# Decay attention and two MLPs on one core: natural keys of two super-blocks turned on TensorE instead of loaded

## The chip, the cores and the metric

One core of a Trainium2 chip runs the whole kernel. The metric is the device time of one execution in microseconds (us). Runs of this kernel lie within about half a per cent of each other.

## The reference

The first stage is a linear attention with decay over 2 batches, 8 heads, 768 positions and 64 columns a head, in blocks of 64 positions with a carried state. Its output, 1536 tokens by 512, goes through two MLPs of inner width 2048, all in float32.

```python
for b in range(nb):                                    # 12 blocks of 64 positions
    qb, kb, vb = (q[:, :, sl], k[:, :, sl], v[:, :, sl])
    intra = np.einsum('bhic,bhjc->bhij', qb, kb) * Dmask[None]
    intra = np.einsum('bhij,bhjd->bhid', intra, vb)
    inter = np.einsum('bhid,bhde->bhie', qb * lam_pow[None], kv_state)
    out[:, :, sl] = intra + inter
    rev_pow = lam[:, None, None] ** (block - 1 - pos[None, :, None])
    kb_dec = kb * rev_pow[None]
    kv_state = lam_block[None, :, None, None] * kv_state + np.einsum('bhsd,bhse->bhde', kb_dec, vb)
...
h = x @ w_in;  g = h * np.clip(h + 3.0, 0.0, 6.0) / 6.0;  x = g @ w_out     # first MLP
h = x @ w_in2; g = np.maximum(0.01 * h, h);               x = g @ w_out2    # second MLP
```

So the keys are needed twice: with columns along the contraction for the scores, and with positions along the contraction for the state.

## The kernel before

The attention goes over six super-blocks u of 128 positions (two blocks of 64). Both batches are worked on at once. For each super-block the input holds queries and keys transposed (columns on the partitions; batch 0 on partitions 64 to 127, batch 1 on 0 to 63), the keys once more in natural order (positions on the partitions), and the values. They are loaded on SP's queue, 256 or 512 KB an issue, at most seven units in flight, in the order of the list LOAD_ORDER (L49): queries with transposed keys ("q"), natural keys ("k", not for the last super-block), values ("v"), with two slices of MLP weights in between. Buffers: three each of QK, NK and the value tile.

TensorE's work for a super-block comes in pieces, whose order is the list PE_ORDER (L52):

- "s" (L390), scores in two halves: 16 f32 matmuls of the interleaved transposed keys (the stationary side, 64 rows by 128 columns) with the queries (128 columns), into two PSUM tiles "pair", of which there are two buffers. The keys are first interleaved into the tile ki by ScalarE (L363). VectorE then multiplies with the decay mask (L402) into r and frees the "pair" buffer.
- "t" (L411), the state: 16 matmuls of natural keys and values. The natural keys are first multiplied with the powers of the decay by GpSimd (L374). VectorE (L423; ScalarE for u = 0) adds the decayed old state. The PSUM tile is one of two of the tag "a".
- "i" (L432), the intra part for batch 0 and batch 1, in PSUM tiles "h" and "a"; "e" (L440), the inter part, added in the same tiles. The result is written as a high part by ScalarE (L451) and a low part by VectorE (L449), batch 0 first.
- "w" (L315), once: the powers of the decay, spread over the partitions. "m" (L656): the first matrix product of the first MLP, standing between the last scores and the last intra part.

The order on the other engines comes from a planner (class Order, L60). It plays the kernel through with costs and due times of its own, starts on each engine what is ready and due first, and writes the instructions in that order. The table PE_US gives it the costs of TensorE's pieces. A load in LOAD_ORDER waits for the one before it. After the attention TensorE runs the MLPs' products (L656, L744, L832) while ScalarE and VectorE unpack the weights and apply the gates.

Of the kernel before, what the change touches and what calls it, by code (L numbers as in the profile page):

```python
# [9 lines left out]
F32 = mybir.dt.float32  # L10
# [4 lines left out]
ALU = mybir.AluOpType  # L15
PSUM = bass.MemoryType.PSUM

B, H, S, D = 2, 8, 768, 64
# [5 lines left out]
P = 128  # L24
# [12 lines left out]
NSB = NSC // 2  # L37
HG = H // 2
SBT = 2 * C
# [4 lines left out]
NQ = 3  # L44
# [1 line left out]
DUE_C = {(0, 0, 0): 25.0, (0, 0, 1): 41.0}  # L46

IN_FLIGHT = 7
LOAD_ORDER = [(n, u) for u in range(NSB) for n in ("q", "k", "v") if (n, u) != ("k", NSB - 1)]  # L49
LOAD_ORDER[16:16] = [(0, 0, 1)]  # L50
LOAD_ORDER[9:9] = [(0, 0, 0)]
PE_ORDER = [("s", 0, 0), ("s", 0, 1), ("w", 0), ("w", 1), ("t", 0), ("i", 0, 0), ("i", 0, 1)]  # L52
for u in range(1, NSB):
    PE_ORDER += [("s", u, 0), ("s", u, 1)] + [("e", u - 1)] * (u > 1)
    PE_ORDER += [("t", u) if u + 1 < NSB else ("m", 0), ("i", u, 0), ("i", u, 1)]
PE_ORDER.append(("e", NSB - 1))
PE_US = {"s": 0.92, "w": 0.86, "t": 0.98, "i": 0.98, "e": 0.95, "m": 2.75}


class Order:  # L60
# [7 lines left out]
    def add(self, engines, fn, due=1e9, after=(), takes=(), frees=()):  # L68


        engines = [engines] if isinstance(engines, tuple) else engines
        self.ops.append((engines, fn, due, [a for a in after if a is not None], list(takes), list(frees)))
        return len(self.ops) - 1
# [103 lines left out]
def decay_attention_two_mlps(ctx: ExitStack, tc: tile.TileContext, qkk, vv, lam, w1, w2, out):  # L177
    nc = tc.nc
    eng = {"act": nc.scalar, "dve": nc.vector, "pool": nc.gpsimd}
# [5 lines left out]
    pool = {n: (sb_att if n in ("r", "vs", "qd", "ki") else ctx).enter_context(  # L185
                tc.tile_pool(name=n, bufs=sizes[n], **({"space": PSUM} if n in "ha" else {})))
            for n in sizes}
# [4 lines left out]
    od = Order({**sizes, "q": NQ, "k": NQ, "pair": 2, **{n: 0 for n in late}, **{f"acc{e}": 0 for e in range(4)}})  # L192
    add = od.add

    def new(n, shape, dtype, name=None):
        return pool[n].tile(shape, dtype, tag=name or n, name=name or n)
# [3 lines left out]
    mm = nc.tensor.matmul  # L200
# [23 lines left out]
    due_pe, at = {}, DUE_S  # L224
    for n in PE_ORDER:
        if n[0] == "s" and not n[2]:
# [5 lines left out]
    for n in PE_ORDER:  # L232
        if n[0] == "m":
# [9 lines left out]
    eye = att.tile([P, SBT], F32, name="eye")  # L243
    ones = att.tile([1, P], F32, name="ones")
    decay = att.tile([P, H, SBT], F32, name="decay")
    k_pow = att.tile([P, H], F32, name="k_pow")
# [10 lines left out]
    NK = [x.rearrange("p (b h d) -> p b h d", b=2, h=H)  # L257
          for x in (sums[:, 2 * NB:2 * NB + NB // 2], sums[:, 2 * NB + NB // 2:3 * NB],
                    att.tile([P, NB // 2], F32, name="nk2"))]
# [70 lines left out]
    nothing = lambda _: None  # L330
    VS, QD, KI, R, PA = {}, {}, {}, {}, {}
# [7 lines left out]
    op_scan = [add(("dve", 1.3), scan(g), -100 + g, after=[op_steps]) for g in range(2)]  # L339
# [33 lines left out]
    def k_decay(u, b):  # L373
        return lambda e: eng[e].tensor_tensor(out=NK[u % NQ][:, b], in0=NK[u % NQ][:, b],  # L374
                                              in1=k_pow.unsqueeze(2).to_broadcast([P, H, D]), op=ALU.mult)

    def q_decay(u, c):
        def fn(e):
            if c == 0:
                QD[u] = new("qd", [P, 2, H, C], F32)  # L380
            eng[e].tensor_tensor(out=QD[u][:, c], in0=QK[u % NQ][:, c, 0], in1=q_pow[:, c], op=ALU.mult)
        return fn
# [71 lines left out]
    x_ready, ld, pieces, los_of, hi_of, masks = {}, {}, {}, {}, {}, []  # L454
    for u in range(NSB):
        d, last = DUE_S + SBT_STEP * u, u + 1 == NSB
        ld["q", u] = add(("dma", 3.3), load_q(u), d - 3.0, takes=["q"])
        if not last:
            ld["k", u] = add(("dma", 1.65), load_k(u), d - 1.5, takes=["k"])
        ld["v", u] = add(("dma", 1.65), load_v(u), d, takes=["vs"])  # L460

    def piece(name, fn, **kw):
        pieces[name] = add(("pe", PE_US[name[0]]), fn, due_pe[name], **kw)
        return pieces[name]
# [3 lines left out]
    for g in range(2):  # L468
        w = piece(("w", g), powers(g), after=op_scan, takes=["h"] + ["a"] * g)
        w_done.append(add(("act", 0.6), powers_copy(g), after=[w], frees=["h"] + ["a"] * g))  # L470
    att_ops = [op_warm, *w_done]
    st_ready, inters, states = {}, {}, {}
    for u in range(NSB):
        d, last = DUE_S + SBT_STEP * u, u + 1 == NSB
        kds = [] if last else [add(("pool", 1.2), k_decay(u, b), due_pe["t", u] - 1.0,
                                   after=[ld["k", u], *op_scan, states.get(u - 2)]) for b in range(2)]
        qds, behind = [], kds[-1] if kds else None
        for c in range(2 if u else 0):
            behind = add(("pool", 1.2), q_decay(u, c), due_pe["e", u] - 1.0, after=[ld["q", u], *w_done, behind],
                         takes=["qd"] * (c == 0))  # L480
            qds.append(behind)
        ki, ms = None, []
        for c in range(2):
            ki = add(("act", 0.6), interleave(u, c), due_pe["s", u, 0] - 1.0, after=[ld["q", u], ki],
                     takes=["ki"] * (c == 0))
        for g in range(2):
            s = piece(("s", u, g), scores_bank(u, g), after=[ld["q", u], ki, op_warm], takes=["pair"])
            ms.append(add(("dve", 1.25), mask(u, g), due_pe["s", u, g] + PE_US["s"], after=[s, op_const], takes=["r"],
                          frees=["pair"]))
        masks += ms  # L490
        add(("none", 0.0), nothing, after=[pieces["s", u, 0], pieces["s", u, 1]], frees=["ki"])
        add(("none", 0.0), nothing, after=[pieces["s", u, 0], pieces["s", u, 1], *qds], frees=["q"])
        if not last:
            t = states[u] = piece(("t", u), state(u), after=[*kds, ld["v", u]], takes=["a"], frees=["k"])
            sl = [add(("act", 0.9), state_decay(u, g), due_pe["s", u, 0],
                      after=[st_ready[u], st_ready.get(u - 1), ki, *w_done]) for g in range(2 if u else 0)]
            st_ready[u + 1] = add(("dve", 0.69) if u else ("act", 0.6), state_next(u), due_pe["t", u] + 1.2, after=[t, *sl, *inters.get(u - 1, [])],
                                  frees=["a"])
            att_ops += [t, *sl, st_ready[u + 1]]
        ins = [piece(("i", u, b), intra(u, b), after=[*ms, ld["v", u]], takes=["ha"[b]]) for b in range(2)]  # L500
        add(("none", 0.0), nothing, after=ins, frees=["r", "r"])
        add(("none", 0.0), nothing, after=[*ins, states.get(u)], frees=["vs"])
        if u:
            ins = inters[u] = [piece(("e", u), inter(u), after=[*ins, *qds, st_ready[u]])]
            add(("none", 0.0), nothing, after=ins, frees=["qd"])
        los, at = [], due_pe["e" if u else "i", u, *[0] * (not u)] + 1.2
        for b in range(2):
            hi = hi_of[u] = add(("act", 0.6), att_x(u, b, False), at, after=ins)
            los.append(add(("dve", 0.69), att_x(u, b, True), at + 0.6, after=[hi], frees=["ha"[b]]))
        if u and not last:  # L510
            for lo in los_of[u - 1]:
                od.ops[lo][3].append(st_ready[u + 1])
        los_of[u] = los
        x_ready[2 * u] = x_ready[2 * u + 1] = add(("none", 0.0), nothing, after=los)
        att_ops += [*ms, *ins, *kds, *qds, *los]
# [88 lines left out]
    for l in range(2):  # L604
        for f in range(NF):
            for j in range(2):
                h = (l, f, j)
# [4 lines left out]
                m = add(("act", 0.67), magnitude(h), early, after=[ld_w, a])  # L612
                kw = dict(frees=["cl"] + ["raw"] * (not (held and f % 2)))
                if h in LOAD_ORDER:
                    x = m
                    for i in range(2):
                        x = add(("dve", 0.8), exponent(h, (i,)), after=[x])
                    x = add(("dve", 0.9), compose(h, (0,)), after=[x])
                    c = add(("dve", 0.9), compose(h, (1,)), after=[a, x], **kw)
                else:  # L620
                    x = add(("dve", 0.85), exponent(h), after=[m])
                    c = add(("dve", 1.4), compose(h), after=[a, x], **kw)
# [3 lines left out]
            if paired(l, f) and f % 2:  # L626
                p, i = f // 2, None
                for n in range(4):
                    i = add(("dve", 0.43), w_sum(l, p, n), after=[composed[l, f - 1, 0], composed[l, f, 0], i])
# [326 lines left out]
    due_p, rest = {}, [("2", 0, 2, starts[0][SINGLE] - i) for i in (2, 1)]  # L956
    for l, b in [(0, b) for b in range(SINGLE, len(BLOCKS[0]))] + [(1, b) for b in range(len(BLOCKS[1]))]:
        fs, end = range(starts[l][b], starts[l][b + 1]), l == 0 and b + 1 == len(BLOCKS[0])
        pair, one, two = (lambda i: ("S", l, fs[i])), (lambda i: ("1", l, fs[i])), (lambda t, i: ("2", l, t, fs[i]))
# [18 lines left out]
        rest = [two(2, i) for i in range(3 if end else 2, 4)]  # L978
# [3 lines left out]
    for s in range(n1 - 2, NS):  # L982
        l, b, t, f = steps[s]
# [313 lines left out]
```

## Time and profile before

| | us |
|---|---|
| median of 3 runs (lowest to highest) | 554.37 (553.35 to 556.07) |
| the profiled execution, device time | 552.44 |
| its span in the trace | 550.7 |
| TensorE busy in the span | 543.3 (99%) |
| VectorE / ScalarE / GpSimd busy | 421.0 / 347.3 / 56.2 |

A busy TensorE is one with a matmul somewhere in flight; matmuls overlap, and short stops between pieces hardly show in it. The page divides the span into 40 slices of 13.8 us; in the trace's answers times count from the span's start.

### The profile page before, as it was taken

What the parts mean: (1) busy time and instruction counts of PE and PEld (TensorE: products, weight loads), DVE (VectorE), ACT (ScalarE), POOL (GpSimd) and SP (SyncE); (2) the same over time, 40 slices, a digit from 0 to 9 for tenths busy, and PEclk for the clock granted to TensorE, in tenths of its full rate; (3) what the DMA queues carried; (4) which work ended last, traced back from release to release, by engine and by line L of the source; (5) the groups of instructions that cost most, each with busy time, mean ns of one, the idle gap of its engine ahead of it and who ended that gap; (6) DMA issues with size and microseconds to landing.
All of it is one profiled execution on the core that took longest, in us unless ns stands there. A gap on an engine that the chain in (4) does not pass through costs nothing.

```text
span 550.7 us, 8354 instructions
## 1 busy us (share of the span) xinstructions
PE 543.3 (99%) x3174; PEld 457.1 (83%) x3174; DVE 421.0 (76%) x711; ACT 347.3 (63%) x629; POOL 56.2 (10%) x62
## 2 busy tenths in 40 slices
PE   9999999999999999999999999999999999999996
PEld 5788888888888788888888888888888888888885
DVE  4778989999989898988689799888287945773342
ACT  4765975678766754687667896686258725573220
POOL 1680002110110110010000000000110110010000
PEclk9999999999999999999999999999999999999999
DMA  8993324455256614342110411341243422411323
GB/s 292 364 341 116 115 79 93 96 140 148 58 120 157 143 44 99 91 159 68 40 39 1 139 52 46 111 151 51 65 114 115 116 57 52 118 22 21 77 66 89
DMA packets 22571, 58.75 MB, mean 107 GB/s; under 512 B 2690, under 2 KB 2946, under 8 KB 22530
## 3 DMA queue, kind: packets, MB, share of 16 engines
q1 hardware_dynamic: 16944, 48.24, 26.9%
q0 software_dynamic: 5184, 9.44, 10.0%
q8 instruction: 25, 0.41, 0.3%
q10 hardware_dynamic: 402, 0.52, 0.3%
q14 instruction: 16, 0.13, 0.1%
HBM read 45.61 MB, written 3.15 MB: 89 GB/s over the span
## 4 chain that ended last, share of the span: by engine, by line
PE 89%; DMA 6%; issue 3%; ACT 1%; SPq 0%; DVE 0%; POOL 0%; ACTq 0%; POOLq 0%
PE acc L744 44%; PE h L832 19%; PE a L832 14%; PE h L656 6%; DMA sums<-qkk 4%; PE a L656 2%; DMA sums<-st 1%; DMA qk<-qkk 1%; PE a L744 1%; PE pair L390 1%; PE h L440 1%; SPq L203 0%; ACT ki L363 0%; PE a L432 0%; PE h L432 0%
## 5 line engine op out<-in xcount | busy, mean ns | idle before, releaser
L699 POOL DMA_DIRECT2D sums<-st x36 | 31.9, 955 | 421.6 <-ACT st L755 421.4
L744 PE MATMUL acc<-Gh,wh 128*128 128x512 f32 x136 | 53.2, 391 | 0.1
L744 PE MATMUL acc<-Gl,wh 128*128 128x512 f32 x136 | 53.1, 390 | 0.0
L744 PE MATMUL acc<-Gh,wl 128*128 128x512 f32 x136 | 52.9, 389 | 0.0
L744 PE MATMUL acc<-wl,Gh 128*128 128x512 f32 x124 | 48.5, 391 | 0.0
L744 PE MATMUL acc<-wh,Gh 128*128 128x512 f32 x124 | 48.4, 391 | 0.0
L744 PE MATMUL acc<-wh,Gl 128*128 128x512 f32 x124 | 48.2, 389 | 0.0
L573 ACT CAST wh<-t 128x512 fp32r<-128x512 f32 (+1 forms) x64 | 37.6, 594 | 16.5 <-DVE t L567 9.2
L541 ACT ACTIVATE c<-raw 128x512 uint32<-128x512 uint32 x64 | 43.1, 673 | 5.4 <-DVE t L567 2.2
L567 DVE CUSTOM_DVE_ANT_0 t<-t,c 128x1024 uint16<-128x1024 uint16 x64 | 44.3, 692 | 2.2
L564 DVE SCALAR_TENSOR_TENSOR t<-raw,t 128x512 uint32<-128x512 uint32 x64 | 44.1, 689 | 1.1
L577 DVE TENSOR_TENSOR wl<-t,wh 128x512 fp32r<-128x512 f32 (+1 forms) x64 | 42.1, 665 | 2.8 <-ACT wh L573 2.8
L757 DVE TENSOR_TENSOR sums<-acc,sums 128x512 f32<-128x512 f32 x35 | 24.0, 690 | 25.7 <-PE acc L744 25.7
L545 ACT ACTIVATE t<-raw 128x512 f32<-128x512 f32 x64 | 42.7, 667 | 0.0
L685 DVE TENSOR_TENSOR Gl<-u,Gh 128x512 fp32r<-128x512 f32 x32 | 22.1, 690 | 23.2 <-ACT Gh L882 23.1
L832 PE MATMUL h<-xh,s 128*128 128x512 f32 x112 | 37.9, 389 | 0.0
L552 DVE TENSOR_SCALAR t<-t 128x512 f32<-128x512 f32 x64 | 27.0, 422 | 9.1 <-ACT t L545 9.1
L744 PEld LDWEIGHTS acc<-Gh,wh 128*128 128x128 f32 x136 | 25.6, 188 | 5.5 <-ACT st L755 0.6
L744 PEld LDWEIGHTS acc<-Gh,wl 128*128 128x128 f32 x136 | 25.5, 188 | 5.4
L755 ACT COPY st<-acc 128x512 f32<-128x512 f32 x34 | 19.9, 588 | 15.7 <-PE acc L744 10.2
L744 PEld LDWEIGHTS acc<-Gl,wh 128*128 128x128 f32 x136 | 25.6, 188 | 4.8
L555 DVE TENSOR_SCALAR t<-t 128x512 uint32<-128x512 uint32 x64 | 27.3, 427 | 2.2
(210 smaller groups left out, 1465.0 us busy)
## 6 DMA issues: line engine op xcount, KB each, us to landing
raw<-w SPq DMA_DIRECT2D x58, 512.0 KB, 3.3
sums<-st POOLq DMA_DIRECT2D x36, 256.0 KB, 4.2
sums<-qkk SPq DMA_DIRECT2D x12, 256.0 KB, 4.1
vs<-vv SPq DMA_DIRECT2D x12, 256.0 KB, 5.2
sums<-qkk SPq DMA_DIRECT2D x6, 512.0 KB, 5.5
raw<-w SPq DMA_DIRECT2D x12, 256.0 KB, 4.2
out<-sums SPq DMA_DIRECT2D x19, 128.0 KB, 2.4
qk<-qkk SPq DMA_DIRECT2D x4, 512.0 KB, 6.4
```

The lines of the kernel that those rows point to most:

```text
L541: nc.scalar.activation(out=CV[h][1], in_=RAW[h][:, :, 0], func=AF.Copy, scale=2.0 ** -29)
L545: return lambda _: nc.scalar.activation(out=CV[h][0].bitcast(F32), in_=RAW[h][:, :, 1].bitcast(F32), func=AF.Abs)
L552: nc.vector.tensor_scalar(out=t.bitcast(F32), in0=t.bitcast(F32), scalar1=MAG_MIN, scalar2=MAG_MAX, op0=ALU.max, op1=ALU.min)
L555: nc.vector.tensor_scalar(out=t, in0=t, scalar1=5, scalar2=2, op0=ALU.logical_shift_left, op1=ALU.logical_shift_right)
L564: nc.vector.scalar_tensor_tensor(out=t, in0=RAW[h][:, :, 1], scalar=0xC0000000, in1=t, op0=ALU.bitwise_and, op1=ALU.bitwise_or)
L567: nc.vector.tensor_tensor(out=t, in0=t, in1=c, op=ALU.add)
L573: nc.scalar.copy(out=W[h][0][:, cols(*h)], in_=CV[h][0].bitcast(F32)[:, cols(*h)])
L577: return lambda e: eng[e].tensor_tensor(out=W[h][1][:, cols(*h)], in0=CV[h][0].bitcast(F32)[:, cols(*h)], in1=W[h][0].bitcast(F32)[:, cols ...
L656: mm(ps, a[:, ws], x[:, k, :], start=(n == 0), stop=(n == 3 * KC - 1))
L699: return lambda _: nc.gpsimd.dma_start(out=SUM[t][:, e, :], in_=STAGE[t, e], accum_op=ALU.add)
L744: mm(ACC[e], a, x, start=(first and n == 0 and not seeded(s, e)), stop=(last and n == 2), skip_group_check=seeded(s, e))
L832: mm(ps, ws[a][:, c * P:(c + 1) * P], xs[b][:, c], start=(first and n == 0), stop=(n == 5), skip_group_check=True)
```

## The change

The natural keys of super-blocks 0 and 1 (TURNED) are no longer loaded. A new piece "x" of TensorE, behind the scores, multiplies the interleaved transposed keys ki (stationary, 128 by 128 per head, both batches at once) with the identity matrix eye: eight f32 matmuls of 128 columns, which put the natural keys into a "pair" tile. VectorE then multiplies them with the powers of the decay out of PSUM (two instructions a super-block, one per batch) into the same tile NK as before; GpSimd's multiplies for these super-blocks go. In these two super-blocks the state piece "t" comes behind the intra pieces. In all super-blocks the result of batch 1 is written ahead of batch 0's, and the rule that a result's low part follows the next state is kept for fewer of them.

```diff
-LOAD_ORDER = [(n, u) for u in range(NSB) for n in ("q", "k", "v") if (n, u) != ("k", NSB - 1)]
...
+TURNED = (0, 1)
+LOAD_ORDER = [(n, u) for u in range(NSB) for n in ("q", "k", "v") if n != "k" or u not in TURNED + (NSB - 1,)]
...
-PE_ORDER = [("s", 0, 0), ("s", 0, 1), ("w", 0), ("w", 1), ("t", 0), ("i", 0, 0), ("i", 0, 1)]
+PE_ORDER = [("s", 0, 0), ("s", 0, 1), ("w", 0), ("w", 1), ("x", 0), ("i", 0, 0), ("i", 0, 1), ("t", 0)]
 for u in range(1, NSB):
     PE_ORDER += [("s", u, 0), ("s", u, 1)] + [("e", u - 1)] * (u > 1)
-    PE_ORDER += [("t", u) if u + 1 < NSB else ("m", 0), ("i", u, 0), ("i", u, 1)]
+    rest = [("t", u) if u + 1 < NSB else ("m", 0), ("i", u, 0), ("i", u, 1)]
+    PE_ORDER += [("x", u), *rest[1:], rest[0]] if u in TURNED else rest
...
+PE_US = {"s": 0.92, "w": 0.86, "t": 0.98, "i": 0.98, "e": 0.95, "m": 2.75, "x": 0.95}
...
+    def turn(u):
+        def fn(_):
+            PA["x", u] = new("pair", [P, H, SBT], F32)
+            ki = KI[u].rearrange("p h i c -> p h (i c)")
+            for h in range(H):
+                mm(PA["x", u][:, h], ki[:, h], eye.rearrange("p (c i) -> p i c", c=2), start=True, stop=True)
+        return fn
+
+    def k_decay_turned(u, b):
+        return lambda e: eng[e].tensor_tensor(out=NK[u % NQ][:, b], in0=PA["x", u][:, :, (1 - b) * D:(2 - b) * D],
+                                              in1=k_pow.unsqueeze(2).to_broadcast([P, H, D]), op=ALU.mult)
...
+        if u in TURNED:
+            x = piece(("x", u), turn(u), after=[ki], takes=["pair", "k"])
+            kds = [add(("dve", 0.69), k_decay_turned(u, b), due_pe["t", u] - 1.0, after=[x, *op_scan]) for b in range(2)]
+            add(("none", 0.0), nothing, after=kds, frees=["pair"])
...
-        for b in range(2):
+        for b in (1, 0):
             hi = hi_of[u] = add(("act", 0.6), att_x(u, b, False), at, after=ins)
             los.append(add(("dve", 0.69), att_x(u, b, True), at + 0.6, after=[hi], frees=["ha"[b]]))
-        if u and not last:
-            for lo in los_of[u - 1]:
-                od.ops[lo][3].append(st_ready[u + 1])
+        if u not in (0, *TURNED, NSB - 1):
+            od.ops[los_of[u - 1][1]][3].append(st_ready[u + 1])
```

On TensorE, in super-blocks 0 and 1, this order stood before (pair<-sums,ki are scores, a<-vs,sums a state, r,vs an intra part):

```order
L390 MATMUL pair<-sums,ki 128x128 x16
L315 MATMUL h<-decay,ones 128x512 x2
L319 MATMUL a<-k_pow,ones 128x8
L411 MATMUL a<-vs,sums 64x64 x16
L432 MATMUL h<-r,vs 64x128 x8
L432 MATMUL a<-r,vs 64x128 x8
L390 MATMUL pair<-sums,ki 128x128 x16
L411 MATMUL a<-vs,sums 64x64 x16
L432 MATMUL h<-r,vs 64x128 x8
L432 MATMUL a<-r,vs 64x128 x8
```

and this stands there now, with the changed kernel's own line numbers (L384 is the turn):

```order
L404 MATMUL pair<-sums,ki 128x128 x16
L317 MATMUL h<-decay,ones 128x512 x2
L321 MATMUL a<-k_pow,ones 128x8
L384 MATMUL pair<-eye,ki 128x128 x8
L446 MATMUL h<-r,vs 64x128 x8
L446 MATMUL a<-r,vs 64x128 x8
L425 MATMUL a<-vs,sums 64x64 x16
L404 MATMUL pair<-sums,ki 128x128 x16
L384 MATMUL pair<-eye,ki 128x128 x8
L446 MATMUL h<-r,vs 64x128 x8
L446 MATMUL a<-r,vs 64x128 x8
L425 MATMUL a<-vs,sums 64x64 x16
```

Eight whole-array matmuls have come in behind the scores in each of the two, and the state has moved behind the intra part.

On VectorE, from the first masks (r<-pair,decay) on, this stood before (state is the state's update, xl the low part of a result):

```order
L402 TENSOR_TENSOR r<-pair,decay 128x1024 x4
L423 TENSOR_TENSOR state_114<-a,state_decayed 128x512
L449 TENSOR_TENSOR xl_121<-h,xh_120 128x4x2x64
L449 TENSOR_TENSOR xl_121<-a,xh_120 128x4x2x64
L402 TENSOR_TENSOR r<-pair,decay 128x1024 x2
```

and now this (sums<-pair,k_pow is the new multiply, t<-t a step of unpacking weights):

```order
L416 TENSOR_TENSOR r<-pair,decay 128x1024 x2
L388 TENSOR_TENSOR sums<-pair,k_pow 128x512 x2
L463 TENSOR_TENSOR xl_121<-a,xh_120 128x4x2x64
L463 TENSOR_TENSOR xl_121<-h,xh_120 128x4x2x64
L416 TENSOR_TENSOR r<-pair,decay 128x1024 x2
L388 TENSOR_TENSOR sums<-pair,k_pow 128x512 x2
L437 TENSOR_TENSOR state_114<-a,state_decayed 128x512
L570 TENSOR_SCALAR t<-t 128x512
L416 TENSOR_TENSOR r<-pair,decay 128x1024 x2
```

The low parts of super-block 0's result now stand ahead of super-block 1's masks; before, they stood behind them and behind the state update.

## Rows read from the trace of the kernel before

**Rows 1.** The page: busy time by engine, and the slices

```profile
PE 543.3 (99%) x3174; PEld 457.1 (83%) x3174; DVE 421.0 (76%) x711; ACT 347.3 (63%) x629; POOL 56.2 (10%) x62
...
PEclk9999999999999999999999999999999999999999
DMA  8993324455256614342110411341243422411323
```

**Rows 2.** Busy time by stage: stretch, length, engines, clock, DMA share, GB/s

```profile
6.77:42.60 35.83, 34.00 (x648) 29.23 (x647) 26.42 (x33) 22.69 (x59) 23.55 (x20) 1.00 0.97 349
42.60:540.00 497.40, 497.18 (x2480) 420.24 (x2477) 389.62 (x667) 321.62 (x566) 31.91 (x36) 1.00 0.33 88
```

**Rows 3.** TensorE in order of time, super-blocks 0 and 1: start, duration

```profile
6.77 2.06 PE L390 MATMUL pair<-sums,ki 64*128 64x128 f32 x32
8.75 1.98 PE L315 MATMUL h<-decay,ones 1*128 1x512 f32 x4
...
10.78 0.33 PE L411 MATMUL a<-vs,sums 128*64 128x64 f32 x2
```

```profile
14.02 2.06 PE L390 MATMUL pair<-sums,ki 64*128 64x128 f32 x32
16.00 1.19 PE L411 MATMUL a<-vs,sums 128*64 128x64 f32 x32
16.98 0.28 PE L432 MATMUL h<-r,vs 128*64 128x128 f32 x1
```

**Rows 4.** TensorE in order of time, around the last super-block

```profile
42.60 0.50 PE L656 MATMUL h<-xh,wh 128*128 128x512 f32 x1
42.93 0.39 PE L656 MATMUL h<-xl,wh 128*128 128x512 f32 x1
43.16 0.40 PE L656 MATMUL h<-xh,wl 128*128 128x512 f32 x1
...
45.56 1.09 PE L432 MATMUL h<-r,vs 128*64 128x128 f32 x16
...
47.46 0.32 PE L440 MATMUL h<-qd,state 64*64 64x128 f32 x1
...
48.49 0.50 PE L656 MATMUL h<-xh,wh 128*128 128x512 f32 x1
```

**Rows 5.** Waits of TensorE's weight loads, 6 to 43 us: total, times, longest

```profile
PEld pair L390 <- ACT ki L363: 2.8, 5, 1.3
PEld a L432 <- DVE state L423: 1.3, 4, 0.6
```

**Rows 6.** ScalarE, then VectorE, in order of time

```profile
17.47 0.69 ACT L363 COPY ki<-qk 128x512 f32<-128x512 f32 x1 [0.63 <-DMA qk<-qkk]
```

```profile
15.22 2.36 DVE L402 TENSOR_TENSOR r<-pair,decay 128x1024 f32<-128x1024 f32 x2 [4.08 <-PE pair L390]
...
18.09 0.68 DVE L449 TENSOR_TENSOR xl<-h,xh 128x512 fp32r<-128x512 f32 x1
18.69 0.68 DVE L449 TENSOR_TENSOR xl<-a,xh 128x512 fp32r<-128x512 f32 x1
```

**Rows 7.** SP's queue in order of time: the fourth group of queries and keys

```profile
24.71 3.88 SPq L203 DMA_DIRECT2D sums<-qkk  x4
```

**Rows 8.** GpSimd in order of time; then a group of the page

```profile
8.96 2.04 POOL L374 TENSOR_TENSOR sums<-sums,k_pow 128x512 f32<-128x512 f32 x2 [7.66 <-DVE k_pow L308]
```

```profile
L757 DVE TENSOR_TENSOR sums<-acc,sums 128x512 f32<-128x512 f32 x35 | 24.0, 690 | 25.7 <-PE acc L744 25.7
```

**Rows 9.** Weight loads of the powers, in order of time

```profile
9.29 0.18 PEld L315 LDWEIGHTS h<-decay,ones 1*128 1x128 f32 x1 [0.24 <-issue]
9.71 0.18 PEld L315 LDWEIGHTS h<-decay,ones 1*128 1x128 f32 x1 [0.24 <-issue]
```

**Rows 10.** Weight loads by form: count, busy us, mean ns

```profile
L656 PEld LDWEIGHTS h<-xl,wh 128*128 128x128 f32 x48 | 9.0, 188 | 1.8
...
L390 PEld LDWEIGHTS pair<-sums,ki 64*128 64x128 f32 x128 | 7.5, 188 | 2.5 <-ACT ki L363 2.5
```

More of the change, by code (lines that the diff above doesn't have):

```diff
@@ L48 @@
 IN_FLIGHT = 7
-LOAD_ORDER = [(n, u) for u in range(NSB) for n in ("q", "k", "v") if (n, u) != ("k", NSB - 1)]
-LOAD_ORDER[16:16] = [(0, 0, 1)]
-LOAD_ORDER[9:9] = [(0, 0, 0)]
-PE_ORDER = [("s", 0, 0), ("s", 0, 1), ("w", 0), ("w", 1), ("t", 0), ("i", 0, 0), ("i", 0, 1)]
+TURNED = (0, 1)
+LOAD_ORDER = [(n, u) for u in range(NSB) for n in ("q", "k", "v") if n != "k" or u not in TURNED + (NSB - 1,)]
+for after, h in ((("v", 2), (0, 0, 0)), (("q", NSB - 1), (0, 0, 1))):
+    LOAD_ORDER.insert(LOAD_ORDER.index(after) + 1, h)
+PE_ORDER = [("s", 0, 0), ("s", 0, 1), ("w", 0), ("w", 1), ("x", 0), ("i", 0, 0), ("i", 0, 1), ("t", 0)]
 for u in range(1, NSB):
     PE_ORDER += [("s", u, 0), ("s", u, 1)] + [("e", u - 1)] * (u > 1)
-    PE_ORDER += [("t", u) if u + 1 < NSB else ("m", 0), ("i", u, 0), ("i", u, 1)]
+    rest = [("t", u) if u + 1 < NSB else ("m", 0), ("i", u, 0), ("i", u, 1)]
+    PE_ORDER += [("x", u), *rest[1:], rest[0]] if u in TURNED else rest
 PE_ORDER.append(("e", NSB - 1))
-PE_US = {"s": 0.92, "w": 0.86, "t": 0.98, "i": 0.98, "e": 0.95, "m": 2.75}
+PE_US = {"s": 0.92, "w": 0.86, "t": 0.98, "i": 0.98, "e": 0.95, "m": 2.75, "x": 0.95}
 class Order:
@@ L457, in decay_attention_two_mlps @@
         ld["q", u] = add(("dma", 3.3), load_q(u), d - 3.0, takes=["q"])
-        if not last:
+        if ("k", u) in LOAD_ORDER:
             ld["k", u] = add(("dma", 1.65), load_k(u), d - 1.5, takes=["k"])
@@ L474, in decay_attention_two_mlps @@
         d, last = DUE_S + SBT_STEP * u, u + 1 == NSB
-        kds = [] if last else [add(("pool", 1.2), k_decay(u, b), due_pe["t", u] - 1.0,
-                                   after=[ld["k", u], *op_scan, states.get(u - 2)]) for b in range(2)]
+        kds = [] if ("k", u) not in LOAD_ORDER else [
+            add(("pool", 1.2), k_decay(u, b), due_pe["t", u] - 1.0, after=[ld["k", u], *op_scan, states.get(u - 2)])
+            for b in range(2)]
         qds, behind = [], kds[-1] if kds else None
@@ L490, in decay_attention_two_mlps @@
         masks += ms
-        add(("none", 0.0), nothing, after=[pieces["s", u, 0], pieces["s", u, 1]], frees=["ki"])
+        if u in TURNED:
+            x = piece(("x", u), turn(u), after=[ki], takes=["pair", "k"])
+            kds = [add(("dve", 0.69), k_decay_turned(u, b), due_pe["t", u] - 1.0, after=[x, *op_scan]) for b in range(2)]
+            add(("none", 0.0), nothing, after=kds, frees=["pair"])
+        add(("none", 0.0), nothing, after=[pieces["s", u, 0], pieces["s", u, 1], pieces.get(("x", u))], frees=["ki"])
         add(("none", 0.0), nothing, after=[pieces["s", u, 0], pieces["s", u, 1], *qds], frees=["q"])
```

## The prediction

> **What bounds the kernel now.** I read the page first: TensorE is busy in 99% of the span, at the full granted clock in all slices, while the DMA row is near full only in the first three or four of 40 slices [rows 1]. So two stretches have to be told apart. The stage windows do that [rows 2]: from 42.60 us, where the first matrix product of the MLPs starts, to 540 us TensorE stands still for next to nothing (497.18 of 497.40 us busy). Whatever moves the start of that product moves the end by as much. In the attention, from the first scores at 6.77 to 42.60 us, the queues are busy 0.97 of the time at 349 GB/s and TensorE still shows 34.00 of 35.83 us. Both are nearly full there, so the question of this change is which of them has more to give.
>
> Busy time hides small stops, so I priced the pieces of TensorE's work by the distance from one start to the next in undisturbed places [rows 3, 4]: the scores of a super-block 1.98 us (14.02 to 16.00), the powers 2.03 (8.75 to 10.78), a state 0.98 (16.00 to 16.98), an intra piece pair 1.90 (45.56 to 47.46), an inter piece 1.03 (47.46 to 48.49). Up to 42.60 us there are six scores, one powers, five states, five intra pairs and four inters: 6 x 1.98 + 2.03 + 5 x 0.98 + 5 x 1.90 + 4 x 1.03 = 32.43 us. The stretch is 35.83 us, so TensorE loses 3.40 us there. The list of waits says to what [rows 5]: 2.8 us on the interleaved keys, which come late because their transfer does (ScalarE stood 0.63 us for one such load at 17.47) [rows 6], and 1.3 us on VectorE's state update (the figures are those of the weight loads, and overlap in part with running matmuls). That is all the change can win on TensorE: 3.40 us, and only as far as the waits come from loads.
>
> **What is removed.** Four loads of 256 KB: 1.05 MB, by the stretch's own 349 GB/s [rows 2] 3.0 us of transfer. Everything that stands behind them on SP's queue moves up by as much, unless a buffer holds it. I checked the buffers of the new order. The natural keys of super-block 4 now wait for the state of super-block 1, which ends near 23.0 us (below); before, their group of issues began at 24.71 [rows 7], 3.0 earlier is 21.7, and the transposed pair goes first. So at most about 1 us is lost of the 3.0, in a load needed some 10 us later. GpSimd loses four multiplies of 1.02 us (from 8.96, 2.04 a pair) [rows 8]; no piece of TensorE waits for GpSimd in [rows 5], so this is worth 0 (if it were all on the path, 4.1 us; nothing points there).
>
> **What is added on TensorE.** Per turned super-block eight matmuls, stationary 128x128, moving 128 columns, both f32. The trace has no such form. A row of an f32 product is half of it: the 16 score matmuls show as 32 rows. The scores run two at a time in two halves of the array, so 1.98 us hold 16 slots of 128 columns: 0.124 us each. The turn has 8 matmuls, 16 rows, and fills the whole array, so nothing runs beside it: 16 slots. Lower bound, from the 512-column product of the powers [rows 9]: its weight loads, one a row, follow each other in 0.42 us (9.29 to 9.71); for 128 columns that is a quarter, 0.105, so 16 x 0.105 = 1.68 us. Upper bounds: a load of 128 columns takes 188 ns [rows 10]; if each can start only when the product before it has begun, a slot is 0.188 and the turn 3.01 us; if only when it has ended, 0.188 + 0.105 and 4.69 us. I take 1.98 us, the row with the same columns, type and number of slots. Twice that is 3.96 us, about double the 0.95 that the kernel's own table gives the piece.
>
> In the MLP products whole-array loads of 188 ns lie beside matmuls that start 0.23 us apart (42.93, 43.16) [rows 4, 10], so there loads overlap running products in the same rows of the array. The Trainium skill (TensorE: Matmul & The Clock Gate, section The mechanism) says that a weight load overlaps matmuls in flight only where its row group differs; a turn uses all rows, so by that rule every slot would be load and product in turn, and two turns would take 9.4 us in place of 3.96, a sum 5.4 us higher. The trace speaks against the rule, at least for 512 columns.
>
> **What is added on VectorE.** Four multiplies out of PSUM, 128x512; the nearest form, the add out of PSUM, takes 690 ns [rows 8]: 2.76 us. VectorE is busy 26.42 of 35.83 us in this stretch [rows 2], so there is room; what counts is the place. The two multiplies of super-block u stand between the masks of u and the state update, and the state piece has been moved behind the intra pieces, whose 1.90 us hide 2 x 0.69 plus the hop. The other added wait: a turn takes one of two "pair" banks, so it waits for the first mask of its own super-block. For u = 0 VectorE is done with the powers when GpSimd starts on them, at 8.96 [rows 8]; the first mask, 1.18 us, ends near 10.1, before 10.78. For u = 1 VectorE's row first has the two subtractions of super-block 0's result, moved ahead of it. Queued behind the waiting turn are the intra pieces, which cannot pass it.
>
> **The walk.** With the prices above: scores 0 from 6.77, powers, turn 0 from 10.78, intra from 12.76, state from 14.66, scores 1 from 15.64 to 17.62. The casts on ScalarE follow the intra's end as before, the two subtractions (started 0.60 apart, 18.09 and 18.69 [rows 6]) end near 16.7; the first mask of super-block 1 starts 1.20 after its scores (14.02 to 15.22), at 16.84, and takes half of 2.36 [rows 6]: 18.02. Turn 1 starts about 18.15, 0.5 us late. Its multiplies end near 21.6, the state piece wants them at 22.03: in time. From there on nothing waits for loads any more: each scores piece comes 1.5 us or more later than before and its keys 2 to 3 us earlier. What remains are stops of about 0.1 us, one per super-block, where the second intra piece waits for a bank that the state update frees (four times in [rows 5]). I take 0.5 + 5 x 0.1 = 1.0 us for the waits left. Bounds: 0.5 if only the mask counts, 3.4 if none of today's goes.
>
> **The sum.** 32.43 + 3.96 + 1.0 = 37.39 us against 35.83: the first MLP product starts 1.56 us later. After it nothing gives that back, because TensorE has no idle time until the tail, and the weights' preparation keeps its place relative to it: behind the last masks VectorE's order is the same but for the batches, and the loads come earlier. The profiled execution is 552.44 us, a span of 550.70 and 1.74 around it: 554.0. The median of the three runs shown is 554.37, 1.93 above the profiled one; carried over, 555.9.
>
> **The other edits.** The order of the batches in writing the result swaps which of two PSUM banks comes free first; the count of instructions is the same. I cost it at 0: it frees first the bank that the next state or intra piece takes. If that is wrong it costs or gains one subtraction's step per super-block it bites, 0.6 us. The dropped order between result and state updates has the same answer, and the same price.
>
> **Rivals.** (1) Slower: the weight load is exposed, so that loads and not columns set the slot. The place is the two turns alone, the price 16 x (0.188 - 0.124) = 1.02 us each, together 2.0: 558.0. It decides (slower by over 0.5%) from a slot of 0.162 us on, since 2.77 - 1.56 = 1.21 us over 32 slots is 0.038. For it: all rows with full 128x128 weights have long moving sides that hide the 188 ns. Against it: the scores reach 0.124 with loads of the same 188 ns. (2) The turn costs what the table says, 0.95: 32.43 + 1.90 + 1.0 = 35.33, 0.5 less than now: 553.9. Against it: no row has 128 f32 columns in 0.06 us on the whole array. The Trainium skill (Perfetto Trace Analysis, section Transposes) advises a transpose proper in place of a standard matmul, since its path skips the arithmetic; the instruction list shows standard ones, and no run here shows the other. (3) Faster: the loads set the pace, and the end comes earlier by the full 3.0 us: 551.4. For it: the queues are 0.97 busy in the stretch. Against it: TensorE's work alone is 32.43 us, and 35.83 - 3.0 = 32.83 leaves 0.4 us for both turns.
>
> **How the numbers follow.** The forecast has 0.64, rival 1 0.17, rival 2 0.15, rival 3 0.04. Half a per cent, 2.77 us, is about what a measurement of this kernel can tell from no change; the forecast is +0.28%, no change that can be told. Same: 0.58 of the forecast (0.06 of it lies over 557.1), 0.14 of rival 2, 0.02 of rival 1: 0.74. Slower: that 0.06 and 0.15 of rival 1: 0.21. Faster: rival 3 and 0.01 of rival 2 by scatter: 0.05. The range: down to 553.6, rival 2 with it and the forecast with a turn of 1.68 (0.6 us less in all); up to 558.2, rival 1 with it. Its ends leave out rival 3, the case that no wait goes, and loads wholly in turn with products.
>
> **What would show it.** Right: turn rows of 128x128 by 128 columns, 16 of them in 1.9 to 2.0 us, twice; hardly any wait of the scores for the interleaved keys after 20 us; a stop near 18 us before the second turn, behind a mask; the first MLP product at about 44.2 us; everything behind it shifted alike. Wrong: that product earlier than 43 us (turns cheaper), later than 45.5 (turns dearer, or the waits stayed), or TensorE idle time between 45 and 540 us, which would mean that the weights' preparation has been pushed out of step.

## The result and the profile after

The changed kernel takes 556.85 us (median of 9 runs, 555.65 to 557.65) beside 554.16 (9 runs, 552.30 to 556.07): ratio 1.0051, interval 1.0037 to 1.0065. It is about half a per cent slower, 2.8 us by the ratio where 1.6 was forecast; the interval lies on both sides of the half per cent that the prediction set between "same" and "slower". Its profiled execution took 555.65 us, 3.21 more than the profiled one before. One run of the experiments below, 3108.8 us with the small edits alone, was slow for no known reason and is left out of its ratio.

TensorE in order of time (start, duration, idle time before and what ended it): the first turn and the piece behind it, the start of the second turn, and the first MLP product:

```profile
11.07 2.45 PE L384 MATMUL pair<-eye,ki 128*128 128x128 f32 x16
13.45 0.77 PE L446 MATMUL h<-r,vs 128*64 128x128 f32 x10
...
18.77 0.40 PE L384 MATMUL pair<-eye,ki 128*128 128x128 f32 x1 [0.43 <-DVE r L416]
...
45.91 0.50 PE L674 MATMUL h<-xh,wh 128*128 128x512 f32 x1
```

A turn lasts from 11.07 to the next piece at 13.45, 2.38 us, and the second one likewise (18.77 to 21.15). It has the 16 rows that were expected, at 0.149 us each and not 0.124. The second turn waits for the mask. The first MLP product stands at 45.91 us, 3.31 later than before [rows 4].

The stages, cut at that product (columns as in [rows 2]):

```profile
7.06:45.91 38.85, 37.69 (x679) 33.51 (x678) 29.20 (x38) 22.50 (x59) 19.23 (x16) 1.00 0.84 300
45.91:540.00 494.09, 494.01 (x2464) 417.57 (x2461) 388.64 (x665) 320.88 (x565) 31.92 (x36) 1.00 0.32 87
```

The queues have fallen from 0.97 to 0.84 of the stretch, and behind the product TensorE has as little idle time as before: nothing is given back. The weight loads' waits from 6 to 46 us:

```profile
PEld a L446 <- DVE state L437: 1.4, 3, 1.0
PEld pair L384 <- DVE r L416: 0.6, 1, 0.6
PEld pair L404 <- issue: 0.6, 2, 0.4
```

The 2.8 us of waits on interleaved keys [rows 5] are gone from the list (0.42 of them lay just ahead of the first scores and so outside the stretch that the prediction summed). One wait has grown: the state update held an intra piece for 1.0 us, where the longest such wait before was 0.6. VectorE and its neighbours show why, at super-block 4:

```profile
39.35 3.03 POOL L395 TENSOR_TENSOR qd<-qk,q_pow 128x512 f32<-128x512 f32 x2 [3.54 <-issue]
39.58 1.64 DVE L595 TENSOR_TENSOR wl<-t,wh 128x512 fp32r<-128x512 f32 x1
...
40.10 1.05 PE L446 MATMUL h<-r,vs 128*64 128x128 f32 x16
...
41.14 0.68 DVE L437 TENSOR_TENSOR state<-a,state_decayed 128x512 f32<-128x512 f32 x1
...
41.87 0.33 PE L446 MATMUL a<-r,vs 128*64 128x128 f32 x2 [0.73 <-DVE state L437]
```

A step of weight preparation (L595) stands ahead of the state update and takes 1.64 us beside a GpSimd multiply that also reads SBUF; the same form took 0.68 at 53.78 us, where GpSimd was idle. The Trainium skill (SBUF — State Buffer, section Who interferes with whom) says that a VectorE tensor_tensor with both inputs in SBUF contends with GpSimd's reads; this row agrees.

### The profile page after: what moved, and what is told of

Read it like the earlier page. It is cut to its first block, busy times and chain, and to the rows that moved or that the text cites. A ratio compares the mean times of both kernels' runs of the same rounds, so it can differ in the third digit from the quotient of the medians.

```text
span 553.8 us, 8408 instructions
## 1 busy us (share of the span) xinstructions
PE 547.3 (99%) x3206; PEld 461.4 (83%) x3206; DVE 423.8 (77%) x715; ACT 346.9 (63%) x629; POOL 51.9 (9%) x58
## 4 chain that ended last, share of the span: by engine, by line
PE 98%; DVE 1%; issue 0%; ACT 0%
PE acc L762 46%; PE h L850 21%; PE a L850 14%; PE h L674 6%; PE a L674 2%; PE pair L404 2%; PE a L446 1%; PE h L272 1%; PE a L762 1%; PE pair L384 1%; PE h L446 1%; PE a L425 1%; PE h L454 1%; DVE r L416 0%; PE h L317 0%; DVE wl L595 0%
## 5 line engine op out<-in xcount | busy, mean ns | idle before, releaser
L595 DVE TENSOR_TENSOR wl<-t,wh 128x512 fp32r<-128x512 f32 (+1 forms) x64 | 42.2, 667 | 2.9 <-ACT wh L591 2.8
```

The source lines that it names most:

```text
L595: return lambda e: eng[e].tensor_tensor(out=W[h][1][:, cols(*h)], in0=CV[h][0].bitcast(F32)[:, cols(*h)], in1=W[h][0].bitcast(F32)[:, cols ...
```

## The experiments

**The loads alone: no turns.** The edit takes the piece "x" and its multiplies out and feeds the two states with values in place of keys.

```diff
-                    mm(ps[other[b], h, :], NK[u % NQ][:, b, h, :], VS[u][:, b, h, :], start=True, stop=True)
+                    mm(ps[other[b], h, :], (VS[u] if u in TURNED else NK[u % NQ])[:, b, h, :], VS[u][:, b, h, :], ...)
```

> The changed kernel without the turns and without the multiplies behind them: the states of super-blocks 0 and 1 are made from the values in place of the keys (so that part of the computation is left out), and the loads stay removed. It shows what the removed loads give by themselves. My theory (TensorE's work of 32.4 us from the first scores to the first MLP product sets the pace, the loads only add waits): the product at 40.8 to 41.6 us, 1.0 to 1.8 earlier than before and 4.3 to 5.1 earlier than in the changed kernel; time 1.0 to 1.8 below before. Rival A (the loads set the pace): the full 3.0 us, product at 39.6. Rival B (the removed loads give nothing): product at 42.3 to 42.9, time as before.

Measured 551.41 us, ratio 0.9954 (0.9942 to 0.9967): 2.5 us below before. The first MLP product:

```profile
41.42 0.50 PE L671 MATMUL h<-xh,wh 128*128 128x512 f32 x1
```

It comes 1.18 us earlier than before, inside the range of my theory. The time gains more than the theory's 1.0 to 1.8, between it and rival A, because the profiled execution of before lies 1.4 us below the median of the runs beside this one (553.80). So the removed loads, with the changed order of pieces and without GpSimd's four multiplies, are worth about 2.5 us, and the changed kernel spends 5.4 on the rest; two turns of 2.38 are 4.8 of that.

**The turn by transpose mode.** One argument:

```diff
-                mm(PA["x", u][:, h], ki[:, h], eye.rearrange("p (c i) -> p i c", c=2), start=True, stop=True)
+                mm(PA["x", u][:, h], ki[:, h], eye.rearrange("p (c i) -> p i c", c=2), start=True, stop=True,
+                   is_transpose=True)
```

> The changed kernel with its two turns done in TensorE's transpose mode; all else is the same. My theory: the turns lie on TensorE's path, and each costs 2.38 us there because a plain f32 product is two rows of weights and columns per head (16 slots of 0.149 us). If the mode needs one row per head, a turn is 8 slots, 0.9 to 1.3 us, and the first MLP product comes 2.2 to 3.0 us earlier than in the changed kernel: at 42.9 to 43.7 us instead of 45.91, time about 554.2, level with the kernel before. Rival (the weight load sets the slot whatever the mode, or the loads from memory set the pace): 16 slots or 2.38 us again, first product at 45.5 to 46.2 us, time as the changed kernel.

Measured 554.11 us, ratio 1.0006 (0.9996 to 1.0016): level with before. TensorE in order of time:

```profile
11.10 1.31 PE L384 MATMUL pair<-eye,ki 128*128 128x128 f32 x8
12.33 1.09 PE L447 MATMUL h<-r,vs 128*64 128x128 f32 x16
...
43.92 0.50 PE L675 MATMUL h<-xh,wh 128*128 128x512 f32 x1
```

Eight rows in place of 16, 1.23 us in place of 2.38, the first product 1.99 us earlier than in the changed kernel (2.2 at the least was expected). Twice 1.15 us is 2.3; the times differ by 0.45%, 2.5 us. So the turn lies on the path, in the times wholly; in the traces 0.3 of the 2.3 us came back as a longer stop in super-block 3, whose intra pieces took 2.32 us in place of 2.05. The advice that the prediction quoted for its rival 2 (the Trainium skill, Perfetto Trace Analysis, section Transposes) holds here.

**The small edits alone**, in the kernel before:

```diff
-        for b in range(2):
+        for b in (1, 0):
...
-        if u and not last:
-            for lo in los_of[u - 1]:
-                od.ops[lo][3].append(st_ready[u + 1])
+        if u not in (0, 0, 1, NSB - 1):
+            od.ops[los_of[u - 1][1]][3].append(st_ready[u + 1])
```

> The kernel before with only the two small edits: batch 1's result written first, and the dropped order between result and state updates. My theory: worth nothing, the first MLP product at 42.3 to 42.9 us as before (42.60), time within 0.5 us. Rival: these edits are behind the loss, the product 1 us or more later, time 1 us or more above before.

Measured 553.64 us, ratio 0.9994 (0.9982 to 1.0006): nothing, as forecast. In the profiled execution (554.16 us), though, the product stands at 44.25 us, where the rival had it. TensorE by stretches (the granted clock is the third number from the end):

```profile
9.00:11.00 2.00, 2.00 (x11) 1.00 (x12) 1.94 (x2) 0.84 (x2) 1.80 (x2) 0.99 0.98 307
11.00:13.00 2.00, 2.00 (x38) 2.00 (x36) 0.00 (x0) 0.58 (x3) 0.00 (x0) 0.50 1.00 390
13.00:15.00 2.00, 2.00 (x28) 2.00 (x27) 0.00 (x0) 2.00 (x6) 0.52 (x1) 0.66 0.81 274
15.00:17.00 2.00, 2.00 (x37) 1.83 (x35) 0.50 (x1) 2.00 (x7) 2.00 (x3) 1.00 1.02 310
```

From 11 us on the clock is at its lower level of 1.2 GHz, and from 15 us on at the full one again. The second scores start at 15.29 us, 1.27 later than before. That is no effect of the edit, for runs of the kernel before have as low a mean clock: see the last section. Behind it the edit does show, with a stop in super-block 1:

```profile
20.10 0.66 PE L432 MATMUL h<-r,vs 128*64 128x128 f32 x8 [1.24 <-DVE r L402]
```

VectorE's order now has the two low parts of super-block 0's result between the two masks of super-block 1, and the intra piece waits for the second mask. The waits on the state update (1.3 us before) are gone from its list in return. The edits move stops, and in the times this comes to nothing.

**The weight step behind the state update**, in the changed kernel:

```diff
+    od.ops[low[0, 0, 0]][3].append(st_ready[NSB - 1])
```

> The changed kernel with one order more: the low part of the first weight slice (1.64 us on VectorE beside a GpSimd multiply) comes after the last state update. My theory: in the changed kernel this instruction delays the state update and so holds the second intra piece of super-block 4 by 0.7 to 0.9 us; without it the first MLP product comes 0.6 to 0.9 us earlier, at 45.0 to 45.3 us, and the time is some 0.7 lower. Rival: the stop only moves, to the weights of that product or to the masks of super-block 5, and the product stays at 45.7 to 46.1 us.

Measured 556.12 us, ratio 1.0040 (1.0025 to 1.0055). The point estimate is 0.6 us below the changed kernel's 1.0051; the intervals overlap, so the time alone doesn't show it. The trace shows the stop gone from its place. TensorE at super-block 4, and the product:

```profile
41.38 1.05 PE L446 MATMUL h<-r,vs 128*64 128x128 f32 x16
42.26 0.94 PE L446 MATMUL a<-r,vs 128*64 128x128 f32 x14
```

```profile
46.25 0.50 PE L676 MATMUL h<-xh,wh 128*128 128x512 f32 x1
```

The second intra half starts 0.88 us after the first, not 1.77. The product's place (46.25) is later than both expectations because this execution also had the low clock, in its first turn, which took 3.54 us; counted from the intra piece behind that turn it comes 31.90 us later (46.25 - 14.35) against 32.46 (45.91 - 13.45), 0.56 less. The stop that went was 0.9 us; some 0.35 of it came back at super-block 3, where the intra pieces took 2.40 us in place of 2.05. There another unpacking step stood ahead of the masks beside a GpSimd multiply (30.66 to 32.88 us), and it took twice its 0.69 us of the changed kernel:

```profile
32.02 1.42 DVE L582 SCALAR_TENSOR_TENSOR t<-raw,t 128x512 uint32<-128x512 uint32 x1
```

The weight step itself took 0.81 us in its new place.

**What sets a turn's 0.149 us a slot.** Two cuts: each head's product in two halves of 64 rows with the 64 columns that matter, side by side in the array; and whole-array products that move 64 columns.

```diff
+                for b in range(2):
+                    r = other[b]
+                    mm(PA["x", u][:, b, h], ki[r, h], eye.rearrange("p (c i) -> p i c", c=2)[r, r.start // 2:r.stop // 2],
+                       start=True, stop=True)
```

```diff
+                mm(PA["x", u][:, h, :D], ki[:, h], eye.rearrange("p (c i) -> p i c", c=2)[:, :D // 2], start=True, stop=True)
```

> The changed kernel with each turn cut in 16 plain products, one per head and batch: stationary 64x128, moving the 64 columns of the identity that aren't zero there, the two batches in two halves of the array and two PSUM banks. It gives the same keys. Theory L (the weight loads of 128 columns set the slot of a short product): two loads side by side in a slot of about 0.124 us as in the scores, though the columns are half: a turn takes 1.9 to 2.1 us. Theory C (the moving columns and a fixed part set it): half the columns, 1.0 to 1.3 us. Time: by L 0.5 to 0.9 below the changed kernel, by C 2 below.

> The changed kernel whose turns move only the first 64 of the identity's 128 columns, with the same stationary 128x128 keys; the keys of one batch are used for both, so that part is left out. Theory L (the loads set the slot): the turn stays at 2.2 to 2.4 us (slots of 0.14 to 0.15). Theory C (columns plus a fixed part): 16 x (0.149 - 0.053) = 1.5 us. A look at the turn alone; its time is not compared.

The halves of rows: 556.26 us, ratio 1.0048 (1.0030 to 1.0065). The median is 0.6 us below the changed kernel's, within L's 0.5 to 0.9, but by the ratios it is 0.2 and the intervals don't tell the two apart; its first MLP product stands at 45.17 us, 0.74 earlier. Its turn in order of time, and then that of the half columns (a single run of 558.03 us, with the low clock elsewhere):

```profile
11.14 2.01 PE L386 MATMUL pair<-eye,ki 64*128 64x64 f32 x32
13.07 1.09 PE L449 MATMUL h<-r,vs 128*64 128x128 f32 x16
```

```profile
11.30 2.01 PE L384 MATMUL pair<-eye,ki 128*128 128x64 f32 x16
13.23 1.08 PE L446 MATMUL h<-r,vs 128*64 128x128 f32 x10
```

Both turns take 1.93 us, 0.121 a slot, with half the columns and so half the streaming. For the halves that is theory L. For the half columns neither theory holds: L said 2.2 to 2.4, C 1.5. So 0.121 is a floor that columns don't move, and the loads of 128 columns (183 to 192 ns each in all of these) are what every slot still has; with 128 columns the whole array needs 0.028 more. By this reading the loads overlap the products, for a load and a product in turn would be 0.293 a slot, but not fully. No run changed the load alone, but the state piece of the changed kernel comes near to it:

```profile
15.25 1.10 PE L425 MATMUL a<-vs,sums 128*64 128x64 f32 x32
16.28 2.06 PE L404 MATMUL pair<-sums,ki 64*128 64x128 f32 x32
```

It moves 64 columns as both cuts do, but loads 64 in place of 128. Its 32 rows run two at a time, 16 slots in 1.03 us, 0.064 a slot: half the load, about half the slot. So the floor is most likely the load's. The state uses the array in two halves of columns, so this isn't a clean test.

**Three stops removed at once**: transpose mode, the late weight step, and the first mask of super-block 1 ahead of super-block 0's low parts.

```diff
+        if u == 1:
+            for lo in los_of[0]:
+                od.ops[lo][3].append(ms[0])
```

> The changed kernel with the turns in transpose mode, the first weight slice's low part behind the last state update, and the first mask of super-block 1 ahead of the low parts of super-block 0's result (so that the second turn needn't wait for them). My theory: TensorE's work from the first scores to the first MLP product is then 32.4 + 2 x 1.24 = 34.9 us and the three stops (0.5, 0.7 to 0.9) are gone: the product 1.0 to 1.6 us earlier than with transpose mode alone (43.92), at 42.3 to 42.9 us, and the time 1.0 to 1.6 below that kernel's 554.11, some 0.9 to 1.5 below before. Rival: the stops move to other places (a landing load, the masks), the product stays above 43.4 us and the time level with before.

Measured 553.86 us, ratio 0.9997 (0.9984 to 1.0011), product at 43.96: the rival. The planner put the low parts between the two masks, and the wait moved to the intra piece (h). And the second turn (pair) still waited:

```profile
PEld h L447 <- DVE r L417: 1.1, 2, 0.7
PEld pair L384 <- DVE r L417: 0.6, 1, 0.6
```

The scores of super-block 1 on TensorE, and the first mask on VectorE:

```profile
15.39 2.06 PE L405 MATMUL pair<-sums,ki 64*128 64x128 f32 x32
```

```profile
16.60 1.22 DVE L417 TENSOR_TENSOR r<-pair,decay 128x1024 f32<-128x1024 f32 x1 [2.64 <-PE pair L405]
```

So the mask's place behind the low parts was not what held the turn: the mask comes 1.2 us after the scores' start in any order (16.28 to 17.49 in the changed kernel, 14.02 to 15.22 before), and lasts 1.2.

**Other work in that gap**: transpose mode and the late weight step again, with VectorE's order left alone and the state of super-block 0 moved between the scores and the turn of super-block 1.

```diff
+PE_ORDER.remove(("t", 0))
+PE_ORDER.insert(PE_ORDER.index(("x", 1)), ("t", 0))
```

> Both super-blocks turned in transpose mode, the first weight slice's low part behind the last state update, and the state piece of super-block 0 between the scores and the turn of super-block 1. The order of masks and results on VectorE is the changed kernel's again. My theory: the second turn's stop of 0.5 us is the mask's own latency (scores half, hop, 1.2 us of mask), so only other work of TensorE can hide it: the state's 1.0 us does, the stop goes, and the first MLP product comes 34.9 us plus at most 0.9 after the first scores, at 42.2 to 42.9 us; time 1 us or more below before, about the kernel that turns super-block 0 alone (552.76). Rival (the late state moves the wait: ScalarE's copy of it, or the bank it holds): the product at 43.3 us or later, time within 0.5 us of before.

Measured 552.98 us, ratio 0.9983 (0.9970 to 0.9995): 0.8 us faster than before, between the theory's 1 and the rival's 0.5. The stop is gone, state and turn follow without idle time:

```profile
17.38 1.15 PE L428 MATMUL a<-vs,sums 128*64 128x64 f32 x32
18.46 1.31 PE L386 MATMUL pair<-eye,ki 128*128 128x128 f32 x8
```

The product stands at 43.60 us, above the expected 42.9 and past the rival's 43.3, in an execution whose clock was at 0.50 from about 12.2 to 15.6 us. How much of the gain over transpose mode alone (1.0006) is the filled gap's and how much the late weight step's, no run shows apart.

**One turn only**, in transpose mode with the late weight step, and then the same with the plain product (late weight step too). The edit is `TURNED = (0,)`.

> As the transpose-mode kernel with the late weight part, but super-block 0 alone is turned; super-block 1's natural keys are loaded again, as before. My theory: TensorE's work is 33.7 us, and half of the transfer is back (1.5 us), so that some waits for the interleaved keys return: product at 42.0 to 43.2 us, time 0.5 to 1.5 below before, within 0.7 of turning both. Rival (TensorE's work alone decides): 1.2 us earlier than turning both, time 2 us or more below before. Rival (loads alone decide): 1.5 us later than turning both, time as before.

> As the kernel that turns super-block 0 alone, but with the plain f32 product of the changed kernel in place of transpose mode. My theory (the turn lies wholly on TensorE's path): 1.1 us later in the first MLP product and in time, 553.9, level with before. Rival (with one turn only, the waits for loads that are left hide part of it): 0.3 us or less, some 553.0.

Transpose mode: 552.76 us, ratio 0.9976 (0.9963 to 0.9988), the lowest of the complete versions, though not apart from the filled gap's 552.98; it is 0.24% (1.4 us) below before, as expected, and 1.1 below turning both (553.86), where at most 0.7 was expected. Plain: 553.83 us, ratio 1.0001 (0.9987 to 1.0015), level with before, as expected. Their first MLP products:

```profile
41.98 0.50 PE L677 MATMUL h<-xh,wh 128*128 128x512 f32 x1
```

```profile
42.65 0.50 PE L676 MATMUL h<-xh,wh 128*128 128x512 f32 x1
```

The medians differ by 1.1 us (1.4 by the ratios), the turn's difference of 1.15 again, so with one turn nothing hides it either. The products can't show this size: the plain execution started its scores 0.80 us earlier and had the low clock in its turn.

## Why the prediction was right, and where it was off

The direction and the mechanism were right: TensorE's own work had no room for the turns, and the shift of the first MLP product passed to the end undiminished. The size was not. That product came 3.31 us later, twice the 1.56 forecast, and at 45.91 us it is past the 45.5 that the prediction named as a sign of being wrong, "turns dearer, or the waits stayed": the turns were dearer, and where the waits for loads went, a new one came. In 11 of the 12 profiled executions of this study the time less that product's start is 509.7 to 510.1 us (552.44 - 42.60 = 509.84 before, 555.65 - 45.91 = 509.74 after, 551.41 - 41.42 = 509.99 without turns); in the twelfth, the half columns, it is 510.52. The sum's terms, from the two traces (the waits before and after are each what is left of a stretch when the pieces' prices are taken off):

| term | predicted, us | measured, us |
|---|---|---|
| two turns | 3.96 | 4.76 |
| waits before, taken off | -3.40 | -3.40 |
| waits after | 1.0 | 1.66 |
| start of the first scores | 0 | 0.29 |
| first MLP product | 1.56 | 3.31 |

Measured waits are 45.91 - 7.06 - 32.43 - 4.76 = 1.66. The pieces' prices held: a state 1.03, an inter 1.03, scores 1.98 in the trace after.

- **The turn was mis-sized** by 0.40 us each: I took the scores' slot of 0.124, in which two half-height loads run in parallel, and a whole-array slot is 0.149. The upper bounds (0.188 and 0.293) were not reached. So the quoted rule that loads overlap only products of other row groups is not borne out as the prediction quoted it: wholly in turn would have been 0.293. The same section also names a load into the background weight buffer as a case that is pulled ahead, which the prediction left out; no run here tells whether these loads are that case.
- **Rival 1** had the right place and, on average, the right side: its load was exposed by four tenths of what it priced (0.025 of 0.064 a slot). Rival 2's 0.95 was not the plain product's price; transpose mode comes nearer to it (1.23). Rival 3 is refuted by the changed kernel; without turns the loads' removal gave 2.5 of its 3.0 us.
- **The waits left** were too small in one place: the walk gave each of five super-blocks 0.1 us for the state update's bank, and at super-block 4 a step of weight preparation ahead of that update made it 0.9. The trace before had such a step beside GpSimd (1.46 us at 30.12) and with it the 0.6 that [rows 5] gives as the longest of the four waits, but the walk didn't carry it. In the weight-step experiment this stop goes and the product gains 0.56, since a part comes back elsewhere.
- **The stop before the second turn** had the right size (0.5) and the right cause in the walk, the mask that starts 1.20 us after its scores. It was only later, in the three-stops experiment, that I put it down to the low parts moved ahead of the mask; that was wrong.
- **The small edits** were worth nothing in time, as priced, though in their own kernel they move stops. GpSimd's relief was priced at nothing too; no run shows it apart from the removed loads.
- **The nearness of the time is in part luck.** On the profiled executions 554.0 us was forecast and 555.65 came, 1.65 too little; for the median 555.9 and 556.85, 0.9 too little. The 1.93 us that the prediction carried over from profile to median were 1.20 in the changed kernel, and this hid 0.7 of the miss. 552.44 us was a low execution of the kernel before, 1.7 below its median; since the time behind the first product hardly varies, the typical execution probably spent more in the attention than the trace that the sum is built on, but none of those was profiled.

## What to carry to other kernels

Before trading a transfer for work on an engine, price the engine's pieces from start to start: 95% busy there left 3.4 us of stops, and removing 3.0 us of transfer won 2.5 of time, less than the 4.8 that two plain turns cost. A transpose by a plain f32 product costs twice what transpose mode does (2.38 against 1.23 us for eight 128x128); one turn in transpose mode, with the weight step moved, gained where two plain ones lost. Where a wait ends on a result that has its own latency, reordering the engine that makes it only moves the stop; other work in the gap removes it.

## What the runs showed of the hardware

The granted clock fell to 0.50, its 1.2 GHz level, in five of the 12 profiled executions (the small edits alone, the late weight step, the half columns, the filled gap, one plain turn) and in none of the other seven, with much the same work. It fell between 10.8 and 13.6 us and was full again between 14.2 and 17.0. Ahead of the drop TensorE was busy without a stop and had run the powers, products with a single row of weights, as in all twelve. In the late-weight-step execution this cost the first turn 1.16 us (3.54 in place of 2.38).

The spread of the kernel before goes with it in part. Of its 74 runs that were taken beside the experiments, 39 had a mean granted clock of 0.997 or less and a median of 554.37 us; the other 35, 553.18. Those 35 alone still spread from 552.23 to 555.70 us, and what makes that was not tried, nor what makes the clock fall in one execution and not in the next. The first scores' start also scatters, from 6.39 to 7.30 us, and the 0.29 us in the table above lie within that.
